# Last group of a two-layer kernel: block 0 from halves, blocks 1 and 2 through partial rows in DRAM, eight first products copied into the other bank

## The chip, the cores and the metric

The kernel runs on one core of a Trainium2 chip. Its engines run side by side, each with its own queue of instructions taken in order: TensorE (PE in the rows, its weight loads PEld), VectorE (DVE), ScalarE (ACT), GpSimd (POOL) and SyncE (SP). SP and POOL issue DMAs; the 16 DMA engines of the core carry them out. The metric is the device time of one execution in microseconds, the median of several runs.

## The reference

```
state = gamma * state + outer(k_t, v_t);  y_t = scale * q_t @ state      # 2 batches, 8 heads, 768 steps, 64 wide
x = y as 1536 tokens x 512                                               # float32 throughout
h = x @ w_in (512 x 2048);   g = h * clip(h + 3, 0, 6) / 6;  x = g @ w_out (2048 x 512)
h = x @ w_in2;               g = h * tanh(softplus(h));      out = g @ w_out2
```

The two matrix layers make up nearly all of the arithmetic. Their first products are x @ w_in, their second products g @ w_out.

## The kernel before

Everything is held transposed: features on the 128 partitions, tokens along the row. The 1536 tokens are three blocks (0, 1, 2) of 512. The 2048 inner features are 16 tiles of 128, two tiles to a pair, two pairs to a group: four groups, 0 to 3, in each layer. A float32 factor is split into a high and a low part (`gh` and `gl`, or `wbh1` and `wbl1` for every third one, on the operand side; `wdh`, `wdl` or the sums in `sb` on the weight side), and a product is three passes on TensorE: high by high, low by high, high by low.

Blocks 1 and 2 together, and the two halves of block 0 by themselves, are multiplied by a scheme of seven products in place of eight; the names end in 1 to 7. `up_pair` makes the first products. For blocks 1 and 2 (`who` is "w") product 1 goes into a PSUM bank `wx`, ScalarE copies it to SBUF (`snap`), product 2 goes into a bank `wy`, and VectorE adds that bank to the copy (`plus`, line 933, the task `c11`), ahead of the activation function.

The second products of a group come in one of three forms. `pair_down` handles blocks 1 and 2 by seven products for each of two pairs and two output tiles: 84 matmuls of 512 columns. `block_down` handles block 0 plainly: 48 matmuls of 512 columns (the last three of them cut in two). `half_down` handles block 0 by its two halves, with the seven products: 84 matmuls of 256 columns. The tuple `HD` names the groups of layer 1 whose block 0 is taken from halves: groups 1 and 2. Group 3, the last one, takes `pair_down` first and then `block_down`.

The groups of layer 1 add up. In groups 0 to 2 ScalarE copies a finished bank to a row tile in SBUF (`copied`, line 1057), and a DMA brings that tile into `part`, a tensor in DRAM of 3 blocks by 4 output tiles of 128 x 512: the first time with a plain write by SP, afterwards with an accumulating DMA issued by POOL (`into_part`, line 1071). There are eight row tiles, taken in turn. In group 3 `read_back` loads all twelve tiles of `part` into SBUF (`xah` and `xal` for blocks 1 and 2, `xch` for block 0), VectorE adds each bank to its tile (`into_back`, line 1063), and SP stores the sums to the output (line 1098). A row of blocks 1 and 2 is stored when its last product is in.

What stands where in each engine's queue is set by a planner (`Plan.order`): for the first part of the program by a written list of names (`SEQ`), after that greedily, by costs and ranks that are constants of the file. So an edit in one place changes the order of neighbouring work elsewhere. Each tile of SBUF or PSUM is handed out in the planned order, and a wait stands where one engine needs what another made.

Of the kernel before, what the change touches and what calls it, by code (L numbers as in the profile page):

```python
# [23 lines left out]
P = 128  # L24
# [8 lines left out]
TB = UPB * P  # L33

NG = 4
# [32 lines left out]
ORDER = (1, 5, 6, 3, 7, 2, 4)  # L68
WP = (1,)
PG = (1, 2)  # L70
HD = (1, 2)
MORE = True
APART = 2
DEFER = {11: 5}
# [177 lines left out]
def body(ctx: ExitStack, tc: tile.TileContext, aps: dict, out: bass.AP):  # L252
    nc = tc.nc
# [639 lines left out]
    def up_pair(who, layer, p):  # L893
        X, Z, Y = wk("x"), wk("y"), wk("y")
        nm = f"{who}{layer}_{p}"
        forms = tform[layer, who]
        if who == "w":
            pass_us, first, last = MMR, slice(0, TB), slice(0, TB)
            g11, g12, g21, g22 = [gbuf(layer, 2 * p + k, b) for k in range(2) for b in (1, 2)]
        else:  # L900
            pass_us, first, last = MMH, slice(0, TB // 2), slice(TB // 2, TB)
            g11, g21 = [gbuf(layer, 2 * p + k, 0) for k in range(2)]
            g12, g22 = g11, g21
        n = first.stop

        def product(k, ps, start, cols, extra):
            l, r = PROD[k]
            which, q = LHS[l]
            if which == 0:
                lh, ll, _ = wbase[layer, 2 * p]  # L910
                ldeps = wbase[layer, 2 * p][2] + wbase[layer, 2 * p + 1][2]
            else:
                lh, ll, lt = wsum[layer, p]
                ldeps = [lt]
            (rh, rhk, rht), (rl, rlk, rlt), rdeps = forms[r]

            def run():
                m = 0
                for kc in range(2):
                    ws = slice(256 * q + kc * P, 256 * q + (kc + 1) * P)  # L920
                    xh, xl = rh.tile[:, rhk.start + kc, rht], rl.tile[:, rlk.start + kc, rlt]
                    for a, c in ((lh, xh), (ll, xh), (lh, xl)):
                        mm(ps.tile[:, cols], a.tile[:, ws], c, start and m == 0, m == 5)
                        m += 1
            return add(f"P{k}_{nm}", "PE", 6 * pass_us, ldeps + rdeps + extra,
                       list(dict.fromkeys([lh, ll, rh, rl, ps])), run, pe_rank[who, layer, p, k])

        def snap(k, ps, pc, gb, gc, dep):
            return add(f"s{k}_{nm}", "ACT", act(n), [dep] + (att_tasks if gb.tag[:2] == "gs" else []), [ps, gb],
                       lambda: A.copy(gb.tile[:, gc], ps.tile[:, pc]))  # L930

        def plus(k, ps, pc, gb, gc, deps):
            return add(f"c{k}_{nm}", "DVE", dve(n), deps, [ps, gb], lambda: V.tensor_tensor(
                out=gb.tile[:, gc], in0=ps.tile[:, pc], in1=gb.tile[:, gc], op=ALU.add),
                pe_rank[who, layer, p, {11: 2, 12: 3, 22: 7}[k]] + 6 * pass_us + (FREE0 if p < NP and who == "w" and k == 11 else FREE) if layer == 1 else None)
        ahead = []
        if layer == 0 and who == "v" and p // NP in PG and p // NP % 2 and p % NP == 0:
            ahead = [up_t["w", 0, p + NP - 1, k] for k in (2, 3, 4)]
        p1 = product(1, X, True, first, ahead)
        s1 = snap(1, X, first, g11, first, p1)  # L940
        if seq_of(who, layer, p) == EARLY_Y:
            p2 = product(2, Y, True, first, [p1])
            p5 = product(5, Z, True, last, [p2])
        else:
            p5 = product(5, Z, True, last, [p1])
            p2 = product(2, Y, True, first, [p5])
        s5 = snap(5, Z, last, g22, last, p5)
        c11 = plus(11, Y, first, g11, first, [p2, s1])
        p6 = product(6, X, False, first, [s1, p1])
        s2 = snap(2, X, first, g12, last, p6)  # L950
        p3 = product(3, Z, False, last, [s5, p5])
        c12 = plus(12, Z, last, g12, last, [p3, s2])
        p7 = product(7, X, False, first, [s2])
        c22 = plus(22, X, first, g22, last, [p7, s5])
        p4 = product(4, X, False, first, [c22])
        f = 2 * p
        if who == "w":
            gval[layer, f, 1] = (g11, [mish_or_swish(f"{layer}_{f}_1", layer, g11, [c11])])
            gval[layer, f, 2] = (g12, [mish_or_swish(f"{layer}_{f}_2", layer, g12, [c12])])
            gval[layer, f + 1, 2] = (g22, [mish_or_swish(f"{layer}_{f + 1}_2", layer, g22, [c22])])  # L960
            gval[layer, f + 1, 1] = (g21, [mish_or_swish(f"{layer}_{f + 1}_1", layer, g21, [p4], src=X)])
        else:
            gval[layer, f, 0] = (g11, [mish_or_swish(f"{layer}_{f}_0", layer, g11, [c11, c12])])
            gval[layer, f + 1, 0] = (g22, [mish_or_swish(f"{layer}_{f + 1}_0d", layer, g22, [c22], last),
                                           mish_or_swish(f"{layer}_{f + 1}_0c", layer, g22, [p4], first, X)])
        for k, t in ((1, p1), (2, p2), (3, p3), (4, p4), (5, p5), (6, p6), (7, p7)):
            up_t[who, layer, p, k] = t
# [67 lines left out]
    back = {}  # L1035
    spares, landed = {}, {}

    def copied(layer, nm, ac, dep, rk):
        if layer not in spares:
            own = [buf("fix", [P, 512], f"sb0{d}") for d in range(4)]  # L1040
            if layer == 0:
                pass
            else:
                wide = buf("fix", [P, 1024], "q")
                own += [buf("fix", [P, 512], "t"), buf("fix", [P, 512], "qc"), View(wide, 0, 512), View(wide, 512, 512)]
            spares[layer] = own
        tp = spares[layer][taken[0] % len(spares[layer])]
        taken[0] += 1
        if layer:
            before = sum([tform[1, w][n][2] for w in "wv" for n in ("T1", "T2", "T3", "T4")], [])  # L1050
        else:
            before = []
            if tp not in spares[layer][:4]:
                before = sum([tform[0, w][n][2] for w in "wv" for n in ("T1", "T2", "T3", "T4")], [])
        sc = 1.0 if layer else 1.0 / 6.0
        return tp, add(f"ev{layer}{nm}", "ACT", act(512), [dep, landed.get(tp)] + before, [ac, tp],
                       lambda: A.activation(tp.tile, ac.tile, AF.Copy, scale=sc), rk)  # L1057
# [14 lines left out]
                out=pt.tile, in_=tp.tile, accum_op=ALU.add))  # L1072

    def read_back(b):
        whole = buf("fix", [P, 2048], ("xch", "xah", "xal")[b])
        for d in range(4):
            v = View(whole, 512 * d, 512)
            pt = part[1, b, d]
            back[b, d] = (v, [add(f"pr{b}_{d}", "SP", 0.8, [added[1, b, d]], [v, pt], lambda v=v, pt=pt:
                                  nc.sync.dma_start(out=v.tile, in_=pt.tile))])  # L1080
# [21 lines left out]

    def pair_down(g, layer=1):
        ps = range(g * NP, (g + 1) * NP)
        final = layer == 1 and g == NG - 1
        pd, z = ("pd", "") if layer else ("pd0", "0")
        gt, gd, sd = {}, {}, {}
        if layer == 0 and g == 2 and MORE:
# [42 lines left out]
        for k in ORDER:  # L1151
# [21 lines left out]
            for d in range(2):  # L1173
                ac, rk, nm = accs[banks[k][d]], rank_after(k, d), f"{z}{g}_{k}_{d}"
                dd = 2 * half + d
                if final:
                    into_back(nm, ac, b, dd, [last[d]], rk, k in (3, 7, 2, 4))
                    ev[banks[k][d]] = back[b, dd][1] if k not in (3, 7, 2, 4) else []
                elif k == 3:
                    tp, t = kept[d]  # L1180
                    t = joined(nm, ac, tp, slice(0, 512), [last[d], t], rk, None if layer else 1.0 / 6.0)
                    into_part(layer, nm, tp, b, dd, t)
                else:
                    tp, t = copied(layer, nm, ac, last[d], rk)
                    ev[banks[k][d]] = [t]
                    if k == 6:
                        kept[d] = (tp, t)
                    else:
                        into_part(layer, nm, tp, b, dd, t)

    def half_down(g):
        ps = range(g * NP, (g + 1) * NP)
# [13 lines left out]
        def form(k):  # L1206
# [6 lines left out]
            for p, c in zip(ps, hs):  # L1213
# [14 lines left out]
                prev_split[0] = a  # L1228
                seen[p, n] = [low[-1]]
            return gh, gl, low  # L1230
        free = sum([tform[1, w][n][2] for w in "wv" for n in ("T1", "T2", "T3", "T4")], [])
        accs, last, ev = {}, {}, {}
        banks = {k: (0, 1) if k in (1, 6, 7, 4) else (2, 3) for k in ORDER}
# [128 lines left out]
    for g in range(NG):  # L1362
        for key in flow1[g]:
            need(key)
        if g == NG - 1:
            for b in (1, 2, 0):
                read_back(b)
        for what in AFTER[g]:
            (pair_down if what == "p" else half_down if g in HD else block_down)(g)

# [71 lines left out]
```

## Time and profile before

| | |
|---|---|
| median of 3 runs | 530.24 us (529.26 to 533.11) |
| profiled execution, its own time | 528.86 us |
| its span, first to last instruction | 527.1 us |
| TensorE busy | 521.0 us, 99% of the span |
| VectorE busy | 447.2 us, 85% |
| ScalarE busy | 356.0 us, 68% |
| GpSimd busy | 58.0 us, 11% |
| granted TensorE clock | 0.998 of full speed |
| DMA, mean | 150 GB/s |

A busy share says how long an engine had an instruction in hand. Matmuls overlap, so their distance from start to start is the price of one, not their duration. VectorE and ScalarE instructions overlap a little with their neighbours too. The share of the DMA engines is the time that their packets took, over 16 engines; it can pass 1 when packets overlap.

### The profile page before, as it was taken

The numbers are of one execution on the slowest core, as the hardware profiler recorded it, in microseconds if no ns is written. First come the engines' busy times: TensorE is split into PE (matmuls) and PEld (weight loads), VectorE is DVE, ScalarE is ACT, GpSimd is POOL, SyncE is SP. The second block draws the span as 40 slices with busy tenths as digits, with TensorE's granted clock in tenths as the row PEclk, the third lists the DMA queues.
The fourth block names the chain that finished last, engine by engine and source line by source line (L and its number), as shares of the span: only waits on it lengthen the run. The fifth ranks groups of instructions, "written<-read, shape, count | busy, mean of one in ns | idle before, by whom it ended". The sixth has DMA issues, their size and how long they took to land.

```text
span 527.1 us, 8602 instructions
## 1 busy us (share of the span) xinstructions
PE 521.0 (99%) x3186; PEld 444.7 (84%) x3186; DVE 447.2 (85%) x745; ACT 356.0 (68%) x646; POOL 58.0 (11%) x70
## 2 busy tenths in 40 slices
PE   8999999999999999999999999999999999999996
PEld 5888888888889888888888898888998899888885
DVE  4999998799998969778889999977899879987892
ACT  3488496757786666686655777776768778786540
POOL 1000000001330020340000000020024300540000
PEclk9999999999999999999999999999999999999999
DMA  8995115443994362798530024682149941995532
GB/s 329 406 410 196 29 52 168 159 156 92 175 193 124 134 139 35 147 127 267 195 130 2 0 81 140 220 199 100 63 116 150 241 133 32 183 123 116 188 137 105
DMA packets 27179, 78.92 MB, mean 150 GB/s; under 512 B 3024, under 2 KB 4432, under 8 KB 27136
## 3 DMA queue, kind: packets, MB, share of 16 engines
q1 hardware_dynamic: 17920, 61.58, 32.3%
q0 software_dynamic: 9216, 16.78, 22.1%
q8 instruction: 25, 0.41, 0.3%
q14 instruction: 18, 0.15, 0.1%
HBM read 52.13 MB, written 26.21 MB: 149 GB/s over the span
## 4 chain that ended last, share of the span: by engine, by line
PE 97%; DMA 1%; DVE 1%; issue 0%; DVEq 0%
PE acc L285 50%; PE wx L285 26%; PE wy L285 21%; DMA kv<-in_kv_dram 1%; DVE A L687 0%; DVE vp L680 0%; DVE xch L1063 0%; DVEq L1437 0%; DVE t L494 0%; DVE bias L266 0%; DVEq L680 0%
## 5 line engine op out<-in xcount | busy, mean ns | idle before, releaser
L285 PE MATMUL acc<-gh,wdl 128*128 128x512 f32 (+1 forms) x216 | 82.6, 382 | 0.0
L285 PE MATMUL acc<-gh,wdh 128*128 128x512 f32 (+1 forms) x216 | 82.5, 382 | 0.0
L285 PE MATMUL acc<-gl,wdh 128*128 128x512 f32 (+1 forms) x216 | 82.3, 381 | 0.0
L1071 POOL DMA_DIRECT2D part<-sb x42 | 37.6, 937 | 387.9 <-ACT sb L1057 294.5
L285 PE MATMUL acc<-gh,sb 128*128 128x512 f32 (+1 forms) x204 | 57.1, 365 | 0.0
L285 PEld LDWEIGHTS acc<-gl,wdh 128*128 128x128 f32 x216 | 40.6, 188 | 7.9
L612 DVE TENSOR_TENSOR cv<-cv 128x256 f32<-128x256 f32 x108 | 45.5, 422 | 1.6
L285 PEld LDWEIGHTS acc<-gh,wdh 128*128 128x128 f32 x216 | 40.7, 188 | 7.2
L285 PEld LDWEIGHTS acc<-gh,wdl 128*128 128x128 f32 x216 | 40.7, 188 | 7.1
L979 ACT CAST gh<-g 128x512 fp32r<-128x512 f32 x54 | 33.5, 621 | 18.0 <-PE acc L285 13.7
L981 DVE TENSOR_TENSOR gl<-g,gh 128x512 fp32r<-128x512 f32 x54 | 37.2, 688 | 9.8 <-PE acc L285 4.8
L285 PEld LDWEIGHTS acc<-gh,sb 128*128 128x128 f32 x204 | 36.5, 189 | 5.9
L554 DVE SCALAR_TENSOR_TENSOR cv<-raw,top 128x1024 int32<-128x1024 int32 (+1 forms) x34 | 39.3, 1157 | 0.4 <-ACT top L549 0.2
L285 PE MATMUL acc<-gl,sb 128*128 128x512 f32 (+1 forms) x102 | 37.1, 364 | 0.0
L979 ACT CAST gh<-gs 128x512 fp32r<-128x512 f32 x43 | 26.7, 620 | 14.9 <-PE acc L285 14.1
L1057 ACT ACTIVATE sb<-acc 128x512 f32<-128x512 f32 x52 | 30.9, 600 | 6.5 <-PE acc L285 5.7
L549 ACT ACTIVATE top<-raw 128x1024 f16<-128x1024 bf16 (+1 forms) x25 | 32.1, 1283 | 1.1 <-DMA raw<-in_w_dram 1.1
L981 DVE TENSOR_TENSOR gl<-gs,gh 128x512 fp32r<-128x512 f32 x43 | 29.6, 688 | 3.4 <-ACT gh L979 2.8
L565 DVE SCALAR_TENSOR_TENSOR wdl<-cv,wdh 128x512 fp32r<-128x512 f32 x32 | 21.6, 686 | 7.6 <-ACT wdh L563 7.3
L285 PE MATMUL wy<-xbh,wsh 128*128 128x512 f32 x60 | 23.5, 392 | 0.0
L285 PE MATMUL wy<-xbh,wsl 128*128 128x512 f32 x60 | 23.4, 390 | 0.0
L285 PE MATMUL wx<-q,wsh 128*128 128x512 f32 x60 | 23.3, 389 | 0.0
(252 smaller groups left out, 1459.0 us busy)
## 6 DMA issues: line engine op xcount, KB each, us to landing
raw<-in_w_dram SPq DMA_DIRECT2D x30, 1023.8 KB, 4.8
part<-sb POOLq DMA_DIRECT2D x42, 256.0 KB, 5.0
qk<-in_qk_dram SPq DMA_DIRECT2D x12, 512.0 KB, 7.3
kv<-in_kv_dram SPq DMA_DIRECT2D x10, 516.0 KB, 6.4
part<-sb SPq DMA_DIRECT2D x18, 256.0 KB, 2.1
part<-q POOLq DMA_DIRECT2D x10, 256.0 KB, 4.9
q<-part SPq DMA_DIRECT2D x8, 256.0 KB, 6.1
raw<-in_w_dram SPq DMA_DIRECT2D x4, 511.8 KB, 7.9
```

The lines of the kernel that those rows point to most:

```text
L285: nc.tensor.matmul(o, l, r, start=start, stop=stop, skip_group_check=True)
L549: a1 = add(nm + "t", "ACT", act(n) * 1.33, [ld, top_free[0]], [rb, t_b], lambda: A.activation(top(), high(), AF.Copy, scale=0.5))
L554: top_free[0] = add(nm + "o", "DVE", dve(n), [a1], [rb, t_b, cb], lambda: V.scalar_tensor_tensor(out=cb.tile.bitcast(I32)[:, cs], in0=low( ...
L565: return add(nm + "lo", "DVE", dve(n), [a], list(dict.fromkeys([cb, hb, lb])), lambda: V.scalar_tensor_tensor(out=lb.tile[:, l0:l0 + n], i ...
L612: prev = [add(nm + f"s{o}", "DVE", dve(256), prev, [cb], lambda o=o, x=x, y=y, op=op: V.tensor_tensor(out=q(o), in0=q(x), in1=q(y), op=op))]
L979: a = add(f"hi{nm}", "ACT", act(512), deps + [prev_split[0]], [gb, gh], lambda: A.copy(gh.tile, gb.tile))
L981: lambda: V.tensor_tensor(out=gl.tile, in0=gb.tile, in1=f32(gh.tile), op=ALU.subtract))
L1057: lambda: A.activation(tp.tile, ac.tile, AF.Copy, scale=sc), rk)
L1071: landed[tp] = added[layer, b, d] = add(f"pa{nm}", "POOL", ADDED, [dep, added[layer, b, d], *more], [tp, pt], lambda: nc.gpsimd.dma_start( ...
```

## The change

Three edits. First, `HD` gains group 3: the second products of block 0 in the last group are made by `half_down`, whose branch for the last group adds each 128 x 256 bank to the tile that was read back into `xch` and stores half rows. Second, `pair_down` loses its branch for the last group: blocks 1 and 2 of group 3 go the way of the other groups, by ScalarE copies and accumulating DMAs into `part`, and SP then copies each finished tile of `part` from DRAM to the output in DRAM; only block 0 is read back. Third, for the eight pairs of layer 0 and layer 1 in `ONTO`, product 1 is copied by ScalarE into the `wy` bank instead of SBUF, product 2 is accumulated onto it by TensorE, and the VectorE addition is gone; the activation function reads the bank.

```diff
+ONTO = ((0, 2), (0, 3), (0, 5), (0, 6), (0, 7), (1, 3), (1, 5), (1, 7))
-HD = (1, 2)
+HD = (1, 2, 3)
...
+        onto = who == "w" and not early and ((layer, p) in ONTO)
...
-        s1 = snap(1, X, first, g11, first, p1)
+        s1 = snap(1, X, first, Y if onto else g11, first, p1)
...
-            p2 = product(2, Y, True, first, [p5])
+            p2 = product(2, Y, not onto, first, [p5] + ([s1] if onto else []))
...
-        c11 = plus(11, Y, first, g11, first, [p2, s1])
+        c11 = p2 if onto else plus(11, Y, first, g11, first, [p2, s1])
...
-            gval[layer, f, 1] = (g11, [mish_or_swish(f"{layer}_{f}_1", layer, g11, [c11])])
+            gval[layer, f, 1] = (g11, [mish_or_swish(f"{layer}_{f}_1", layer, g11, [c11], src=Y if onto else None)])
...
-        whole = buf("fix", [P, 2048], ("xch", "xah", "xal")[b])
+        whole = buf("fix", [P, 2048], "xch")
...
-        final = layer == 1 and g == NG - 1
...
-                if final:
-                    into_back(nm, ac, b, dd, [last[d]], rk, k in (3, 7, 2, 4))
-                    ev[banks[k][d]] = back[b, dd][1] if k not in (3, 7, 2, 4) else []
-                elif k == 3:
+                if k == 3:
...
+                if layer and g == NG - 1 and k in (3, 7, 2, 4):
+                    pt = part[1, b, dd]
+                    add(f"y{nm}", "SP", 0.8, [added[1, b, dd]], [pt], lambda b=b, dd=dd, pt=pt: nc.sync.dma_start(
+                        out=out[dd * P:(dd + 1) * P, b * TB:(b + 1) * TB], in_=pt.tile))
...
-            for b in (1, 2, 0):
-                read_back(b)
+            read_back(0)
```

On SP, at the end of the program, before (the reads of `part` in its last four rows, then the stores of sums):

```order
L1080 DMA xah_5149<-part_340_3696 128x512
L1080 DMA xch_5243<-part_335_3474 128x512
L1080 DMA xch_5243<-part_336_3493 128x512
L1080 DMA xch_5243<-part_334_3464 128x512
L1098 DMA out_dram<-xal_5152 128x512 x4
L1098 DMA out_dram<-xah_5149 128x512 x4
L1098 DMA out_dram<-xch_5243 128x512 x3
L1098 DMA out_dram<-xch_5243 128x256 x2
```

The same place now; a `part` row is a tile of blocks 1 or 2 that goes from DRAM to DRAM, an `xch` row a half row of block 0:

```order
L1086 DMA xch_5225<-part_336_3488 128x512
L1194 DMA out_dram<-part_341_3607 128x512
L1194 DMA out_dram<-part_342_3614 128x512
L1194 DMA out_dram<-part_343_3539 128x512
L1277 DMA out_dram<-xch_5225 128x256 x2
L1194 DMA out_dram<-part_337_3507 128x512
L1277 DMA out_dram<-xch_5225 128x256 x4
L1194 DMA out_dram<-part_344_3547 128x512
L1277 DMA out_dram<-xch_5225 128x256 x2
L1194 DMA out_dram<-part_338_3517 128x512
L1194 DMA out_dram<-part_339_3687 128x512
L1194 DMA out_dram<-part_340_3691 128x512
```

Eight reads of `part` into SBUF are gone, the eight stores of blocks 1 and 2 have become eight copies between DRAM tensors, and three of these stand behind the last half rows.

On POOL the queue ended with group 2's accumulations; now twelve more follow, the last eight of them these (`t`, `qc`, `q` and `sb` are the row tiles):

```order
L1077 DMA part_341_3607<-t_3497 128x512
L1077 DMA part_342_3614<-qc_3503 128x512
L1077 DMA part_343_3539<-q_3526 128x512
L1077 DMA part_337_3507<-sb_732_3443 128x512
L1077 DMA part_344_3547<-q_3526 128x512
L1077 DMA part_338_3517<-sb_733_3453 128x512
L1077 DMA part_339_3687<-sb_734_3461 128x512
L1077 DMA part_340_3691<-sb_735_3473 128x512
```

Each of these eight is followed by one copy on SP that waits for it to land.

On VectorE, the last work of the program before (L1063 adds a bank, L981 makes a low part):

```order
L981 TENSOR_TENSOR wbl_989_5396<-wsh_942_4737,wbh_988_5389 128x512
L981 TENSOR_TENSOR gl_5407<-wsh_942_4737,gh_5402 128x512
L1063 TENSOR_TENSOR xah_5149<-acc_950_5106,xah_5149 128x512
L1063 TENSOR_TENSOR xah_5149<-acc_951_5178,xah_5149 128x512
L981 TENSOR_TENSOR gl_5422<-wsl_946_5183,gh_5414 128x512
L981 TENSOR_TENSOR wbl_995_5441<-wsl_946_5183,wbh_994_5436 128x512
L1063 TENSOR_TENSOR xch_5243<-acc_986_5410,xch_5243 128x512
L1063 TENSOR_TENSOR xch_5243<-acc_987_5417,xch_5243 128x512
```

A stretch of the same work now (L1272 adds a bank, L1232 makes a low part, L1210 a difference of the operands):

```order
L1272 TENSOR_TENSOR xch_5225<-acc_986_5422,xch_5225 128x256
L1232 TENSOR_TENSOR gl_5495<-wsh_942_5105,gh_5479 128x256
L1272 TENSOR_TENSOR xch_5225<-acc_987_5438,xch_5225 128x256
L1210 TENSOR_TENSOR wsh_942_5105<-wsh_942_5105 128x256
L1232 TENSOR_TENSOR gl_5495<-wsl_946_5174,gh_5479 128x256
L1210 TENSOR_TENSOR wsl_946_5174<-wsl_946_5174 128x256
L1272 TENSOR_TENSOR xch_5225<-acc_982_5402,xch_5225 128x256
L1232 TENSOR_TENSOR wbl_1001_5528<-wsh_942_5105,wbh_1000_5512 128x256
```

Block 0 takes 36 operations of 256 columns (8 differences, 14 low parts, 14 additions) in place of nine (four low parts and five additions, two of these of 256 columns); the additions for blocks 1 and 2 in group 3 have left VectorE but for two.

## Rows read from the trace of the kernel before

**Rows 1.** The page: busy time by engine, and the chain's shares by engine.
```profile
PE 521.0 (99%) x3186; PEld 444.7 (84%) x3186; DVE 447.2 (85%) x745; ACT 356.0 (68%) x646; POOL 58.0 (11%) x70
PE 97%; DMA 1%; DVE 1%; issue 0%; DVEq 0%
```

**Rows 2.** Waits of TensorE, whole span: total us, times, longest us.
```profile
PE acc L285 <- DVE t L494: 1.2, 1, 1.2
PE acc L285 <- DVE vp L680: 0.3, 1, 0.3
PE wy L285 <- DVE A L687: 0.2, 1, 0.2
```

**Rows 3.** Chain that ended last, in order of time, its last long piece: start, us.
```profile
495.05 27.95 PE acc L285 x126
```

**Rows 4.** Timeline of TensorE: last product of blocks 1, 2; block 0's first and last.
```profile
511.69 0.39 PE L285 MATMUL acc<-gl,wdh 128*128 128x512 f32 x1
511.92 0.39 PE L285 MATMUL acc<-wbh,wdh 128*128 128x512 f32 x1
...
522.59 0.28 PE L285 MATMUL acc<-wbh,wdl 128*128 128x256 f32 x1
522.71 0.28 PE L285 MATMUL acc<-wbl,wdh 128*128 128x256 f32 x1
```

**Rows 5.** Page, costliest groups: ScalarE copies of a finished bank.
```profile
L1057 ACT ACTIVATE sb<-acc 128x512 f32<-128x512 f32 x52 | 30.9, 600 | 6.5 <-PE acc L285 5.7
```

**Rows 6.** Groups of VectorE by shape: additions of a `wy` bank.
```profile
L933 DVE TENSOR_TENSOR gs<-wy,gs 128x512 f32<-128x512 f32 x15 | 10.3, 689 | 4.5 <-PE wy L285 3.1 <-ACT gs L850 0.7 <-PE acc L285 0.7
L933 DVE TENSOR_TENSOR g<-wy,g 128x512 f32<-128x512 f32 x15 | 10.3, 688 | 5.7 <-PE wy L285 5.7
```

**Rows 7.** Timeline of VectorE: two neighbours of 256 columns, in group 2's halves.
```profile
437.33 0.42 DVE L1204 TENSOR_TENSOR wsl<-wsl 128x256 f32<-128x256 f32 x1
437.66 0.42 DVE L1204 TENSOR_TENSOR wsh<-wsh 128x256 f32<-128x256 f32 x1
```

**Rows 8.** Timeline of VectorE and SP at the end, then the window behind the last transfer.
```profile
523.02 0.76 DVE L1063 TENSOR_TENSOR xch<-acc,xch 128x256 f32<-128x256 f32 x2
523.03 1.33 SPq L1098 DMA_DIRECT2D out_dram<-xch  x3
526.00:527.10 1.10, 0.00 (x0) 0.00 (x0) 0.00 (x0) 0.00 (x0) 0.00 (x0) 0.50 0.00 0
```

**Rows 9.** Page, DMA queues (packets, MB, share) and issues (count, KB, us to landing).
```profile
q0 software_dynamic: 9216, 16.78, 22.1%
part<-sb POOLq DMA_DIRECT2D x42, 256.0 KB, 5.0
```

**Rows 10.** DMA queue of POOL in 470 to 476 us, then 422.5 to 424.5 us.
```profile
q0 software_dynamic: 474, 0.86, 103.1%
...
q0 software_dynamic: 205, 0.39, 106.7%
```

**Rows 11.** One accumulating DMA with nothing ahead of it, issued at 466.98 us.
```profile
part<-t POOLq DMA_DIRECT2D x1, 256.0 KB, 4.0
```

**Rows 12.** DMA queue of SP: 484 to 492 (loads), 504 to 516 (stores), 521 to 527.1.
```profile
q1 hardware_dynamic: 1008, 1.84, 70.6%
...
q1 hardware_dynamic: 1146, 2.09, 47.0%
out_dram<-xal SPq DMA_DIRECT2D x4, 256.0 KB, 2.0
...
q1 hardware_dynamic: 720, 1.05, 47.8%
```

**Rows 13.** Both DMA queues busy at once: 410 to 412 us, then 418 to 422 us.
```profile
q1 hardware_dynamic: 85, 0.70, 100.1%
q0 software_dynamic: 3, 0.00, 0.7%
...
q1 hardware_dynamic: 115, 0.94, 72.6%
q0 software_dynamic: 112, 0.20, 28.2%
```

More of the change, by code (lines that the diff above doesn't have):

```diff
@@ L904, in up_pair @@
         n = first.stop
+        early = seq_of(who, layer, p) == EARLY_Y
+        onto = who == "w" and not early and ((layer, p) in ONTO)
         def product(k, ps, start, cols, extra):
@@ L939, in up_pair @@
         p1 = product(1, X, True, first, ahead)
-        s1 = snap(1, X, first, g11, first, p1)
-        if seq_of(who, layer, p) == EARLY_Y:
+        s1 = snap(1, X, first, Y if onto else g11, first, p1)
+        if early:
             p2 = product(2, Y, True, first, [p1])
@@ L1036, in body, with spare @@
     spares, landed = {}, {}
-    def copied(layer, nm, ac, dep, rk):
+    def spare(layer):
         if layer not in spares:
@@ L1046, in copied @@
             spares[layer] = own
+    def copied(layer, nm, ac, dep, rk):
+        spare(layer)
         tp = spares[layer][taken[0] % len(spares[layer])]
@@ L1230, in form @@
             return gh, gl, low
+        spare(1)
         free = sum([tform[1, w][n][2] for w in "wv" for n in ("T1", "T2", "T3", "T4")], [])
```

## The prediction

> **What bounds the kernel now.** I read the busy shares and the chain first: TensorE is busy 99% of the span, and the chain that ended last is TensorE for 97% [rows 1]. A busy share could hide small stalls, so the waits come next: TensorE waited 1.7 us in all, three times, all of it at the start of the program [rows 2]. From start to start the matmuls stand 0.227 us apart at 512 columns and 0.12 us at 256, to the end [rows 4]. So until its last matmul this kernel is TensorE's instruction count; an edit gains there only if it takes matmuls away. Behind it lies a tail: the last matmul starts at 522.71 [rows 4], VectorE's last additions run to 523.78, SP's last store issues at about 523.9 (three issues in 1.33 us, 0.44 us each) and the last transfer has ended by 526.0; 1.1 us without any work closes the span [rows 8]. The chain's last piece covers blocks 1 and 2 and then block 0 of the last group without a gap [rows 3]. I set t = 0 at 511.92, where block 0 begins [rows 4]; the products before it keep their number, so I leave this point where it is. In t, TensorE ends at 10.9, the transfers at 14.1, the span at 15.2.
>
> **The first products onto copied banks.** Eight VectorE additions of 0.69 us go [rows 6], 5.5 us; no matmul comes or goes. VectorE was not what TensorE waited for, so this is worth 0 at the end; what hides it is TensorE's own unbroken work. The new wait: product 2 now needs ScalarE's copy. In the new order of TensorE 18 to 120 matmuls of 512 columns' worth stand between the two in each of the eight places, at least 4.08 us of work by 0.227 us each, and a copy of a bank takes 0.6 us [rows 5]. A copy from bank to bank shows in no row; below zero it cannot gain, and were it three times as slow it would still fit. Behind product 2 all of TensorE would wait, so ScalarE more than 3 us late would cost its lateness. I take 0, with 0 to 2 us for all eight. The `wy` banks are held longer, and the planner has moved neighbouring products for that; I keep the same 0 to 2 us for that.
>
> **Block 0 from halves.** Before: 45 matmuls of 0.227 us and 6 of 0.12 us, 10.9 us. After: 84 of 0.12 us, 10.1 us. TensorE ends at t = 10.1: 0.8 us gained, if it is fed. Feeding: VectorE has 36 operations of 256 columns, 0.335 us from start to start [rows 7], 12.1 us, against 10.1 us on TensorE. It must start early: the operand buffers are three deep, so the first half's low part can start when the third product from the end has been read, 2.7 us before t = 0, and ScalarE's cast (about 0.4 us) is done: t = -2.2. Then VectorE ends at 9.9 at the soonest, and its last addition, which waits for the last matmul, at 10.6. Each half product finds its operands by a margin of tenths. Without the head start TensorE would wait some 2 us. I take 0.1 us; bounds 0 and 2 us.
>
> **Blocks 1 and 2 through `part`.** Eight reads into SBUF go (they ran from 484 us, under TensorE: worth 0), twelve additions of 0.69 us become ScalarE copies of 0.6 us [rows 5]: two to a product of 2.7 us, next to two casts of 0.62 us, so ScalarE keeps up. New are twelve accumulating DMAs and, behind each of the last eight, a copy from DRAM to DRAM.
>
> *When they are issued.* Six products after the first one take 16.3 us up to t = 0, so the banks are copied at about t = -16.3, -15.1 and -13.6, -12.4 (products 1, 5), then at -7.5, -6.9 (3), -5.5, -4.3 (7), -2.7, -1.8 (2) and 0.0, 0.8 (4).
>
> *What one costs.* 9216 packets are 64 accumulating DMAs, 144 each [rows 9]. With only these in hand the DMA engines carried 474 packets in 6 us, 1.82 us for 144, and with a deeper backlog 205 in 2 us, 1.4 us [rows 10]. With its issue, an undisturbed one lands after 4.0 us [rows 11], so its packets start some 1.75 us behind the issue. Here a backlog builds; I take 1.6 us between these two. A load from `part` cost 70.6% of 8 us for 7, 0.81 us; a store of the same size 47.0% of 12 us for 8, 0.71 us; by the last window a half row costs 0.4 us [rows 12]. DRAM to DRAM is in no row. From below it is bounded by the store, 0.71 us (a gain is excluded: it moves the same bytes); from above by the accumulation, 1.82 us, which also reads and writes DRAM. I take the load's 0.81 us, since it is plain and reads DRAM.
>
> *The sum.* The first four accumulations are over by t = -7. From -5.7 on the DMA engines have 8 x 1.6 + 8 x 0.81 + 8 x 0.4 = 22.5 us of work: end at t = 16.8, 17.2 with the last receipt. TensorE and the half rows are done by then: the last half row can be issued at 11.1, three copies behind it at 11.6, 12.0 and 12.5 if their accumulations have landed. So the DMA engines become the bound of the tail.
>
> *How two queues share.* Where both had work, SP's queue carried 85 packets and POOL's 3 in 2 us, but 115 and 112 in another 4 us [rows 13]: once SP's first, once in turns. In turns, the copies thread between the accumulations and the sum above holds: 17.2. If SP's transfers go first, the last accumulation lands last, and its copy follows alone (issue, 0.81 us, receipt): about 18.8. I take 17.5, nearer the first, for the packets here are of one size as in no window of rows 13. The Trainium skill says, in DMA: Bandwidth & Descriptors (Queues, rings and completion order), that each DMA engine goes round its queues packet by packet; by this rule alone the end is 17.2, and the first window of rows 13 does not agree with it.
>
> Result: the span ends at 511.9 + 17.5 + 1.1 = 530.5, 3.4 us later than 527.1. The profiled execution took 528.86 us by its own time, 1.4 us under the median of 530.24; I add the 3.4 us to both: 532.3 for such an execution, **533.6 us** for the median.
>
> **The rivals.** *DMA keeps up* (0.21). Accumulations at 1.4 us and copies at 0.71 us leave 8 x 1.4 + 8 x 0.71 + 3.2 = 20.1 us of work, over at t = 14.4; then the half rows and the three copies behind them set the end: eight transfers of 4.3 us in all, issued from 9.3 on, end at 15.1 to 15.5. Span 528.5, median 531.6; 530.2 if the copies land like stores. For it: a backlog raises the rate. Against it: 1.82 us was the rate in the group just before. The Trainium skill's formula for POOL's DMAs (the same page, Anatomy of one DMA: about 2.0 us plus the bytes over 436 GB/s) gives 2.6 us for a tile, and by it nothing would pile up. An undisturbed landing of 4.0 us [rows 11] is over that.
>
> *Slower: copies or accumulations are dear* (0.26). At 1.82 us for an accumulation with SP's transfers first the end is t = 20.5; with copies at the accumulation's price too, 8 x 1.82 x 2 + 3.2 = 32.3 us from -5.7 give 27. Span 533.5 to 540, median 536.6 to 543. It decides from about 1.1 us a copy at 1.6 us an accumulation. For it: DRAM is read and written at once, and SP's first window. Against it: loads and stores side by side reach 0.7 to 0.8 us.
>
> *TensorE is starved in the halves or at a copied bank* (0.06): 1 to 4 us there. The DMA engines get that time for their backlog, so the end moves less than 2 us: 534 to 536.
>
> *Faster* (0.02): the eight additions were holding something up; 5.5 us and 0.8 us go, 524. No wait in rows 2 speaks for it.
>
> **How the numbers follow.** One per cent, 5.3 us, is about what a measurement of this kernel tells from no change: 524.9 and 535.5 are the bounds. The forecast's own case has 0.45, with 531.6 to 535.5 around 533.6. Slower by over 1%: the dear transfers, 0.26, a third of the starved case, 0.02, and 0.03 from the forecast's upper edge: 0.31. Faster 0.02, within 0.67. The range holds the forecast, most of the first rival, and the second up to copies of 1.3 us: 530.2 to 539.
>
> **What would show it.** Right: in the profile after, TensorE ends near 522 without gaps behind 495, the DMA share stays near 1 from 506 to 529, POOL's last accumulation lands some 12 us after its issue, and the chain ends with a `part` to `out_dram` copy on SP. Wrong: the DMA share falls before 524 and SP's last issue is at 524 (first rival); copies that land 4 us and more after their issue with nothing else in flight (second); gaps on TensorE behind 512 that wait for a low part (third).

## The result and the profile after

The changed kernel took 533.26 us (median of 14 runs, 532.81 to 534.68), the kernel before 529.23 us beside it (14 runs); the ratio is 1.0074, 95% interval 1.0061 to 1.0088. Forecast were 533.6 us, and 3.4 us more than before; it became 3.9 us more by the ratio. The profiled execution took 532.84 us with a span of 531.0 us, against 528.86 and 527.1. So the time was inside the range and near the forecast, in part by luck: the kernel before came out 1.0 us under the 530.24 us that the forecast stood on, and the increase 0.5 us over the forecast one, so the two misses partly cancel. Whether the reason was right is another question, and the experiments answer it differently.

The page of the changed kernel: busy time by engine, and the chain's shares. Then TensorE's waits over the whole span.

```profile
PE 520.6 (98%) x3219; PEld 445.6 (84%) x3219; DVE 443.3 (83%) x752; ACT 364.2 (69%) x668; POOL 68.7 (13%) x82
PE 96%; DMA 1%; DVE 1%; issue 0%; DVEq 0%
```

```profile
PE acc L286 <- DVE t L495: 1.2, 1, 1.2
PE acc L286 <- DVE vp L681: 0.3, 1, 0.3
PE wy L286 <- DVE A L688: 0.2, 1, 0.2
```

Against [rows 1] VectorE has 3.9 us less, ScalarE 8.2 us more, TensorE almost the same. The waits are those of [rows 2] to the tenth: nothing new in 500 us (gaps shorter than these are not in that view). TensorE's timeline around block 0, to set against [rows 4]:

```profile
511.75 0.39 PE L286 MATMUL acc<-gl,wdh 128*128 128x512 f32 x1
512.15 0.38 PE L286 MATMUL acc<-wbh,wdh 128*128 128x256 f32 x1
512.37 0.28 PE L286 MATMUL acc<-wbh,wdl 128*128 128x256 f32 x1
...
522.16 0.28 PE L286 MATMUL acc<-wbh,wdl 128*128 128x256 f32 x1
522.28 0.28 PE L286 MATMUL acc<-wbl,wdh 128*128 128x256 f32 x1
```

Block 0 starts at 512.15, 0.23 us later than before; 0.17 us of it is a gap ahead of the first half matmul (0.40 us behind the one before it in place of 0.227). From the first to the last start pass 10.13 us, and TensorE is through 0.43 us sooner than before. The loss lies behind it. SP's queue from there on (start, time of the group, count):

```profile
518.32 1.12 SPq L1277 DMA_DIRECT2D out_dram<-xch  x2
519.49 0.50 SPq L1194 DMA_DIRECT2D out_dram<-part  x1
520.43 2.37 SPq L1277 DMA_DIRECT2D out_dram<-xch  x4
522.89 0.50 SPq L1194 DMA_DIRECT2D out_dram<-part  x1
523.48 1.02 SPq L1277 DMA_DIRECT2D out_dram<-xch  x2
524.75 2.06 SPq L1194 DMA_DIRECT2D out_dram<-part  x3
```

Before, the last issue was over at 524.36 [rows 8] and the last packet by 525.7, 1.3 us behind it (the first window below). Now the last issue is over at 526.81 (+2.45) and the last packet ends 3.0 us behind it (+1.7): 529.8. Windows behind TensorE, first before, then now, with the DMA share in the column before the last; then SP's wait at the very end:

```profile
525.70:526.00 0.30, 0.00 (x0) 0.00 (x0) 0.00 (x0) 0.00 (x0) 0.00 (x0) 0.50 0.00 0
...
526.80:529.80 3.00, 0.00 (x0) 0.00 (x0) 0.00 (x0) 0.00 (x0) 0.00 (x0) 0.50 0.81 256
529.80:531.00 1.20, 0.00 (x0) 0.00 (x0) 0.00 (x0) 0.00 (x0) 0.00 (x0) 0.50 0.00 0
```

```profile
SPq L1443 <- DMA out_dram<-part: 2.4, 3, 1.2
```

The end is the landing of the three copies that SP issued last. The page's own chain stops at VectorE's last addition and does not show this; SP's waits do.

The DMA queues from 506 to 530 us hold just the eight accumulations, the eight copies and the eight half rows (packets, MB, share):

```profile
q0 software_dynamic: 1152, 2.10, 61.1%
q1 hardware_dynamic: 2304, 3.15, 39.6%
```

POOL's queue carried 14.7 us of packets, 1.83 us an accumulation; SP's 9.5 us, against the 9.7 us of the forecast's prices. In the sum 24.2 us, and the share stays near 1 up to 529. Read by itself, this is the forecast's picture.

### The profile page after: what moved, and what is told of

Same layout as the page of the kernel before. It is cut to its first block, busy times and chain, and to the rows that moved or that the text cites. A ratio compares the mean times of both kernels' runs of the same rounds, so it can differ in the third digit from the quotient of the medians.

```text
span 531.0 us, 8725 instructions
## 1 busy us (share of the span) xinstructions
PE 520.6 (98%) x3219; PEld 445.6 (84%) x3219; DVE 443.3 (83%) x752; ACT 364.2 (69%) x668; POOL 68.7 (13%) x82
## 4 chain that ended last, share of the span: by engine, by line
PE 96%; DMA 1%; DVE 1%; issue 0%; DVEq 0%
PE acc L286 50%; PE wx L286 26%; PE wy L286 21%; DMA kv<-in_kv_dram 1%; DVE A L688 0%; DVE xch L1272 0%; DVE vp L681 0%; DVE t L495 0%; DVE bias L267 0%; DVEq L681 0%
## 5 line engine op out<-in xcount | busy, mean ns | idle before, releaser
L1077 POOL DMA_DIRECT2D part<-sb x50 | 44.4, 955 | 419.6 <-ACT sb L1063 315.1
L286 PE MATMUL acc<-gh,wdl 128*128 128x512 f32 (+1 forms) x212 | 80.6, 380 | 0.0
L286 PE MATMUL acc<-gh,wdh 128*128 128x512 f32 (+1 forms) x212 | 80.6, 380 | 0.0
L286 PE MATMUL acc<-gl,wdh 128*128 128x512 f32 (+1 forms) x212 | 80.4, 379 | 0.0
L286 PE MATMUL acc<-gh,sb 128*128 128x512 f32 (+1 forms) x228 | 61.6, 356 | 0.0
L286 PEld LDWEIGHTS acc<-gh,sb 128*128 128x128 f32 x228 | 40.3, 189 | 5.9
L286 PE MATMUL acc<-gl,sb 128*128 128x512 f32 (+1 forms) x114 | 40.5, 356 | 0.0
L1063 ACT ACTIVATE sb<-acc 128x512 f32<-128x512 f32 x60 | 35.7, 599 | 6.6 <-PE acc L286 5.3
L982 ACT CAST gh<-gs 128x512 fp32r<-128x512 f32 x43 | 26.6, 619 | 13.0 <-PE acc L286 12.5
L286 PEld LDWEIGHTS acc<-gl,sb 128*128 128x128 f32 x114 | 21.5, 189 | 3.1
```

What stands on the lines that cost most here:

```text
L286: nc.tensor.matmul(o, l, r, start=start, stop=stop, skip_group_check=True)
L982: a = add(f"hi{nm}", "ACT", act(512), deps + [prev_split[0]], [gb, gh], lambda: A.copy(gh.tile, gb.tile))
L1077: landed[tp] = added[layer, b, d] = add(f"pa{nm}", "POOL", ADDED, [dep, added[layer, b, d], *more], [tp, pt], lambda: nc.gpsimd.dma_start( ...
```

## The experiments

For a common measure I count from block 0's first matmul on TensorE to the end of the span. The start of the program varies by some us between executions (TensorE's first waits), and this takes it out. Before: 511.92 to 527.1, 15.2 us; changed: 512.15 to 531.0, 18.85 us. These are single profiled executions; the ratios of the experiments to the kernel before come from five rounds each.

| kernel | ratio to before (95%) | block 0's start, span | start to end |
|---|---|---|---|
| changed | 1.0074 (1.0061 to 1.0088) | 512.15, 531.0 | 18.85 |
| banks alone | 0.9991 (0.9982 to 1.0001) | 512.65, 527.7 | 15.05 |
| halves alone | 0.9994 (0.9984 to 1.0003) | 513.09, 527.7 | 14.6 |
| rows alone | 1.0086 (1.0072 to 1.0100) | 512.93, 532.4 | 19.5 |
| onto the output | 0.9969 (0.9958 to 0.9980) | 512.19, 525.9 | 13.7 |
| onto the output, no banks | 0.9969 (0.9952 to 0.9987) | 512.73, 526.4 | 13.7 |
| onto the output, plain block 0 | 0.9990 (0.9971 to 1.0010) | 512.81, 527.8 | 15.0 |
| half copies | 1.0059 (1.0038 to 1.0080) | 513.27, 530.4 | 17.1 |
| last copies on ScalarE | 1.0067 (1.0051 to 1.0083) | 513.55, 531.4 | 17.85 |
| plain writes | 1.0075 (1.0057 to 1.0093) | 513.86, 532.6 | 18.7 |
| plain writes, last copies on ScalarE | 1.0035 (1.0018 to 1.0051) | 512.33, 529.5 | 17.2 |
| plain writes, copies first | 0.9989 (0.9977 to 1.0001) | 514.97, 529.0 | 14.0 |
| copies of block 1 only | 1.0059 (1.0040 to 1.0078) | 512.61, 530.4 | 17.8 |

### Which of the three edits

**Banks alone.** The old last group, with `ONTO` kept:

```diff
-HD = (1, 2, 3)
+HD = (1, 2)
...
+                if final:
+                    into_back(nm, ac, b, dd, [last[d]], rk, k in (3, 7, 2, 4))
...
+            for b in (1, 2, 0):
+                read_back(b)
```

> Only the eight first products go onto copied banks; the last group is as before. My theory (the time went to the DMA engines in the tail): no change, ratio to before 0.998 to 1.002, span 527.1 within 0.5 us, TensorE without waits after the start. Rival (the copied banks or the new order of products cost TensorE time): a ratio over 1.003, with gaps on TensorE ahead of a second product.

Measured: 0.9991, no change. Its span is 0.6 us longer than that of before, 0.1 us more than I had allowed, with a wait of TensorE of 0.8 us for an input at the start that the execution of before did not have. The eight copied banks and the moved products are worth nothing that shows.

**Halves alone.**

```diff
-ONTO = ((0, 2), (0, 3), (0, 5), (0, 6), (0, 7), (1, 3), (1, 5), (1, 7))
+ONTO = ()
...
+                if final:
+                    into_back(nm, ac, b, dd, [last[d]], rk, k in (3, 7, 2, 4))
...
+            for b in (1, 2, 0):
+                read_back(b)
```

> Only block 0 of the last group is made from halves; blocks 1 and 2 are read back and joined as before. My theory: TensorE ends 0.4 us sooner, as it does in the changed kernel (522.56 in place of 522.99), the last half row is issued by about 523.6 and lands 2.0 us later, then 1.1 us: span 526.7, ratio 0.998 to 1.000. Rival (VectorE starves TensorE in the halves, and this is a part of the loss): TensorE ends after 523.5 and the ratio is over 1.002.

Measured: 0.9994, and 14.6 us from the start of block 0 in place of 15.2. From 513.09 to 524.07, where its last matmul starts, TensorE took 11.0 us, not 10.1, and no less than the 10.8 us of plain block 0 [rows 4]: eleven matmuls started about 0.1 us late, against two in the changed kernel.

```profile
524.07 0.28 PE L286 MATMUL acc<-wbl,wdh 128*128 128x256 f32 x1
```

So the rival's sign came true on TensorE (it ends after 523.5), the rival's ratio did not, and what is gained lies behind TensorE. Here VectorE still adds the banks of blocks 1 and 2; that this starves the halves is likely but not shown. The ratio is in the expected range, its interval holds 1: no loss is here, and a gain of half a us can't be told from none.

**Rows alone.**

```diff
-ONTO = ((0, 2), (0, 3), (0, 5), (0, 6), (0, 7), (1, 3), (1, 5), (1, 7))
-HD = (1, 2, 3)
+ONTO = ()
+HD = (1, 2)
```

> Only blocks 1 and 2 of the last group go through the partial rows and are copied to the output; block 0 stays plain, nothing goes onto copied banks. My theory (the tail is the DMA engines' work): the whole loss is here, span 530.4 to 531.2, ratio 1.006 to 1.009. Rival (the loss needs the eight half rows that stand between the copies on SP's queue): five stores in place of eight take two thirds of it away, ratio under 1.004.

Measured: 1.0086, span 532.4: the whole loss, and no less than with the half rows. SP's last groups:

```profile
524.39 1.55 SPq L1104 DMA_DIRECT2D out_dram<-xch  x3
526.04 1.78 SPq L1194 DMA_DIRECT2D out_dram<-part  x3
```

Five stores of block 0 or eight, three copies stand behind them.

### The copies taken away

**Onto the output.** The rows of blocks 1 and 2 of layer 1 are the output's own rows, from the first write of group 0 on:

```diff
+    for b in (1, 2):
+        for d in range(4):
+            part[1, b, d] = Buf(f"out{b}{d}", lambda b=b, d=d: out[d * P:(d + 1) * P, b * TB:(b + 1) * TB])
...
-                if layer and g == NG - 1 and k in (3, 7, 2, 4):
-                    pt = part[1, b, dd]
-                    add(f"y{nm}", "SP", 0.8, [added[1, b, dd]], [pt], lambda b=b, dd=dd, pt=pt: nc.sync.dma_start(
-                        out=out[dd * P:(dd + 1) * P, b * TB:(b + 1) * TB], in_=pt.tile))
```

> The changed kernel with the rows of blocks 1 and 2 of layer 1 held in the output tensor itself: the same accumulating DMAs, but onto the output, and the eight copies from DRAM to DRAM are gone. My theory: the DMA engines have the accumulations (14.7 us of packets from 506.5 on) and the half rows (3.2 us), over at about 523.5 to 524; the last half row sets the end as in the kernel without the rows: span 526.5 to 527.3, ratio 0.998 to 1.001, over 3.5 us faster than the changed kernel. Rival (the accumulations alone bound the tail): the last one lands after 525.5 and the span is 528 or more, ratio over 1.002.

Measured: 0.9969, faster than both kernels, 1.6 us under the kernel before; 13.7 us from block 0's start. POOL's queue from 506 to 524, and SP's last group:

```profile
q0 software_dynamic: 1152, 2.10, 83.3%
```

```profile
518.35 5.24 SPq L1276 DMA_DIRECT2D out_dram<-xch  x8
```

The accumulations cost the same (15.0 us of packets for eight), and yet the tail is shorter than before: the half rows set the end, as expected. It was 0.6 us better than the lower end of my span, and the ratio lies under the range that I gave. This tells that the copies make the loss, not how: by their work or by their place.

**Onto the output, with plain block 0, and without the banks.** The same edit with

```diff
-HD = (1, 2, 3)
+HD = (1, 2)
```

> As the kernel that accumulates onto the output itself, but with block 0 of the last group plain, as before the change. What the half products are worth when the copies are gone: my theory says 0.4 us at TensorE's end and nothing in the tail, so a span of 526.3 to 527.0 against 525.9, ratio to before 0.997 to 0.9995. Rival (the gain of that kernel comes from the half rows being smaller at the very end): span 527.0 or more, ratio 0.9995 or over.

and with

```diff
-ONTO = ((0, 2), (0, 3), (0, 5), (0, 6), (0, 7), (1, 3), (1, 5), (1, 7))
+ONTO = ()
```

> The kernel that accumulates onto the output itself, with the eight first products copied to SBUF and added by VectorE again, as before the change. My theory (the eight additions are off the path): ratio to before 0.996 to 0.999, from block 0's first matmul to the end 13.7 us within 0.4, as with the copied banks. Rival (VectorE needs the 5.5 us to feed the halves): TensorE waits in block 0, ratio 0.9995 or over.

Measured: 0.9990 (0.9971 to 1.0010) with plain block 0, at 15.0 us from its start, and 0.9969 without the banks, at 13.7 us. So the halves are worth about 1.3 us once the copies are gone: 0.7 us on TensorE, the rest behind it. My 0.4 us was too small: the span of 527.8 us is where the rival had it, the ratio where I had it, and the interval touches that of the kernel with the halves. The banks are worth nothing here either.

### By their work or by their place

**Half copies.**

```diff
-                        out=out[dd * P:(dd + 1) * P, b * TB:(b + 1) * TB], in_=pt.tile))
+                        out=out[dd * P:(dd + 1) * P, b * TB:b * TB + 256], in_=pt.tile[:, 0:256]))
```

> The changed kernel with every copy from DRAM to DRAM cut to 256 of its 512 columns: the other half of the rows of blocks 1 and 2 is never written to the output. My theory (work of the DMA engines, in proportion): the eight copies fall from 6.4 us of packets to about 3.2, the span from 531.0 to 528.0 (527.4 to 528.8), ratio to before 1.001 to 1.004. Rival (a chain of latencies: each copy takes its 3.5 to 4 us behind an accumulation's receipt, whatever its size): span 530.4 to 531.2, ratio over 1.006.

Measured: 1.0059, 17.1 us. Neither theory: SP's packets fell from 9.5 to 6.7 us, 2.8 us of work, the time by 1.7 us. SP's queue in 506 to 530 us, then in 526 to 528 us, while the last copies ran:

```profile
q1 hardware_dynamic: 2304, 2.10, 27.8%
...
q1 hardware_dynamic: 358, 0.33, 50.2%
```

With the DMA engines half idle, work no longer bounds that end. What was saved is mostly the landing of a last copy, 2.5 us from its issue in place of 3.9 us.

**Last copies on ScalarE.**

```diff
-                    add(f"y{nm}", "SP", 0.8, [added[1, b, dd]], [pt], lambda b=b, dd=dd, pt=pt: nc.sync.dma_start(
+                    late = k == 4 or k == 2 and d == 1
+                    add(f"y{nm}", "ACT" if late else "SP", 0.1 if late else 0.8, [added[1, b, dd]], [pt], lambda b=b, dd=dd, pt=pt, late=late: (nc.scalar if late else nc.sync).dma_start(
```

> The changed kernel with its last three copies, those that stood behind the last half rows on SP's queue, issued from ScalarE's queue behind its last cast; nothing else is moved. My theory (the DMA engines have no free time between 506 and 529): no gain, span 530.5 to 531.5, ratio to before 1.006 to 1.009. Rival (SP's order holds them back: they were issued at 524.75 to 526.3, up to 2.5 us after their rows had landed): issued by 524, landed by 528, span 528.5 to 529.5, ratio under 1.005.

Measured: 1.0067, as my theory said, but 1.0 us shorter from block 0's start. The copies, then the last half rows, and what SP waited for there:

```profile
521.55 3.38 ACTq L1195 DMA_DIRECT2D out_dram<-part  x3
...
526.87 0.81 SPq L1278 DMA_DIRECT2D out_dram<-xch  x2
```

```profile
SPq L1278 <- DMA out_dram<-xch: 1.1, 1, 1.1
SPq L1278 <- DMA out_dram<-part: 1.0, 1, 1.0
```

Counted from block 0's start, the three copies were all issued by 11.4 us in place of 14.7; now the half rows were last, held by transfers that had not landed. The Trainium skill says, in DMA: Bandwidth & Descriptors (Issuing engines are not separate DMA queues), that issuing on several engines saves only the sequencer's time; this run's ratio agrees, 1.0067 against 1.0074. The same move with plain writes, below, saves more (1.0035 against 1.0075), since it takes the copies from behind half rows that wait for the end; so the sequencer's time is not all that it can save.

**Plain writes.** What became of the main term of my sum, if the accumulations are made cheap:

```diff
-                out=pt.tile, in_=tp.tile, accum_op=ALU.add))
+                out=pt.tile, in_=tp.tile, **({} if nm.startswith("3_") else {"accum_op": ALU.add})))
```

> The changed kernel with the twelve transfers of the last group's rows into the partial rows as plain writes in place of accumulating ones, on the same queue of POOL: the sums of the first three groups are lost for blocks 1 and 2. If the price of an accumulation, 1.83 us of packets, is that DRAM is read and written, a plain write costs 0.7 to 0.8 us like a store, the eight fall by 8 us and the tail is bound by issue and receipt: span 527 to 528.5, ratio to before 0.999 to 1.003. If it is POOL's queue or its 144 packets that cost, nothing changes: 531.0, ratio 1.006 to 1.009.

Measured: 1.0075, 18.7 us. That looks like the second answer, but the trace says otherwise. POOL's queue from 505 to 533, its last issue, and SP's last group:

```profile
q0 software_dynamic: 640, 2.10, 20.6%
```

```profile
515.00 0.54 POOL L1077 DMA_DIRECT2D part<-sb  x1 [0.25 <-ACT gh L1231]
...
526.06 2.08 SPq L1194 DMA_DIRECT2D out_dram<-part  x3
```

Eight transfers took 5.8 us of packets in place of 14.7 (80 packets each, not 144), the last was issued at 515.00, and still the end did not move: 8.9 us of the work that my sum of 22.5 us was made of are gone, for 0.1 us. So that sum alone does not hold the end of the changed kernel. SP's order is enough to hold it: the last three copies were issued behind the last half rows, their rows landed by 519.6. Nor do the accumulations make these copies land later. Their times from issue to landing, in the changed kernel and here:

```profile
DMA to landing us min/median/max: 3.8/3.9/4.1
DMA to landing us min/median/max: 3.5/3.7/4.1
```

**Plain writes, last copies on ScalarE.** Both edits above together; the diff is theirs.

> Both earlier edits at once: the last group's rows go into the partial rows by plain writes (the sums of the first three groups are lost for blocks 1 and 2), and the last three copies are issued from ScalarE's queue. Counted from block 0's first matmul on TensorE the span ended after 18.85 us in the changed kernel, 18.7 with plain writes alone, 17.85 with the three copies moved alone. My theory now (two bounds that lie close together, either of which holds the end: SP's order, with three copies behind the last half rows, and the work of the DMA engines, which the accumulations make up in the main): only with both lifted does the time come back, to 15.0 to 16.0 us, ratio to before 0.999 to 1.003. Rival (a copy between DRAM tensors is late by its own latency wherever it is issued): 17.5 or more, ratio over 1.004.

Measured: 1.0035, 17.2 us, between the two answers. The copies on ScalarE's queue, and the DMA engines in 518 to 520 us:

```profile
520.34 1.95 ACTq L1195 DMA_DIRECT2D out_dram<-part  x3
```

```profile
q1 hardware_dynamic: 143, 0.13, 19.7%
```

The rows lay ready by 518.5, the DMA engines were nearly idle, and the copies stood behind ScalarE's last cast: held by place once more, then bunched with the half rows. The edit had not lifted the bound it was to lift.

**Plain writes, copies first.** The edit of the plain writes, and all eight copies ahead of the half rows on SP:

```diff
-                    add(f"y{nm}", "SP", 0.8, [added[1, b, dd]], [pt], lambda b=b, dd=dd, pt=pt: nc.sync.dma_start(
+                    t = add(f"y{nm}", "SP", 0.8, [added[1, b, dd]], [pt], lambda b=b, dd=dd, pt=pt: nc.sync.dma_start(
...
+                    t.after = ld_last[0]
+                    ld_last[0] = t
...
-                        add("y" + nm, "SP", 0.5, [t], [v], lambda v=v, dd=dd, c=c: nc.sync.dma_start(
+                        y = add("y" + nm, "SP", 0.5, [t], [v], lambda v=v, dd=dd, c=c: nc.sync.dma_start(
...
+                        y.after = ld_last[0]
```

> Plain writes of the last group's rows (the sums of the first three groups are lost for blocks 1 and 2) and all eight copies put ahead of the half rows on SP's queue, so that no copy waits for block 0. The copies then run as soon as their rows have landed, by about 8 us after block 0's first matmul. If place and time of issue set the end and not the copies as such, the end is that of the kernel without copies, 13.7 to 15.2 us after block 0's first matmul, ratio to before 0.997 to 1.001. If copies are dear wherever they stand: 17 us or more, ratio over 1.003.

Measured: 0.9989, 14.0 us. SP's queue:

```profile
509.88 11.67 SPq L1195 DMA_DIRECT2D out_dram<-part  x8
521.65 4.99 SPq L1280 DMA_DIRECT2D out_dram<-xch  x8
```

The same eight copies, all of them done before the first half row has landed, cost next to nothing: 14.0 us against 13.7 without any. This is shown with plain writes only.

**Copies of block 1 only.** Block 2's rows accumulate onto the output; block 1's keep their copies:

```diff
+    for b in (2,):
+        for d in range(4):
+            part[1, b, d] = Buf(f"out{b}{d}", lambda b=b, d=d: out[d * P:(d + 1) * P, b * TB:(b + 1) * TB])
...
-                if layer and g == NG - 1 and k in (3, 7, 2, 4):
+                if layer and g == NG - 1 and k in (2, 4):
```

> The changed kernel with block 2's rows accumulated onto the output itself, so that its four copies are gone; block 1's four rows keep the partial rows and their copies, the ones that stand last on SP. Counted from block 0's first matmul to the end of the span the changed kernel took 18.85 us, and 13.7 us without any copy. If a copy costs by its work, half the copies are half the loss: 16.3 us, ratio to before 1.001 to 1.003. If the last copies set the end by their place (behind the last accumulation and the last half rows on SP, three issues and the landing of the last), nearly all of it stays: 17.5 to 18.5 us, ratio 1.004 to 1.008.

Measured: 1.0059, 17.8 us: half the copies gone, 80% of the loss still there (17.8 less 13.7 of 18.85 less 13.7). SP's last two groups:

```profile
523.68 1.00 SPq L1280 DMA_DIRECT2D out_dram<-xch  x2
524.78 1.14 SPq L1197 DMA_DIRECT2D out_dram<-part  x2
```

Two copies behind the last half rows are enough to hold the end.

## Why the prediction was right, and where its reason was not

**Banks: right.** Worth 0, in two settings (0.9991 alone; 0.9969 with and without them in the kernel without copies).

**Halves: right in the sum, small in the end.** TensorE takes 10.13 us from first to last start, about 10.25 with the last matmul's own 0.12 (10.1 and 0.1 for waits forecast), and ends 0.43 us sooner, 0.17 us being lost in a gap ahead of the first half matmul. The gain is hidden behind the copies.

**Prices: copy and half row right, accumulation short.** Eight copies and eight half rows took 9.5 us of packets (9.7 forecast). An accumulation took 1.83 us, the upper bound, not 1.6: the backlog did not raise the rate.

**Two queues: in turns, as taken.** While both had transfers on their way they carried about as many packets each. In 512 to 514 us:

```profile
q0 software_dynamic: 96, 0.18, 69.3%
q1 hardware_dynamic: 91, 0.17, 26.0%
```

**Issue of the accumulations: wrong.** I had the last banks copied at t = 0 and 0.8 and the accumulations issued at once, so that the last would land some 12 us after its issue. The copies ended at 512.10 and 512.88, as forecast, but POOL issued at 516.51 and 518.49 (ScalarE's last copies, then POOL's last issues, then the last landing in us from its issue):

```profile
511.50 0.60 ACT L1063 ACTIVATE sb<-acc 128x512 f32<-128x512 f32 x1 [0.40 <-PE acc L286]
512.28 0.60 ACT L1063 ACTIVATE sb<-acc 128x512 f32<-128x512 f32 x1
```

```profile
512.12 0.86 POOL L1077 DMA_DIRECT2D part<-sb  x1 [0.41 <-ACT sb L1063]
516.51 0.86 POOL L1077 DMA_DIRECT2D part<-sb  x1 [3.53 <-ACT gh L1231]
518.49 0.88 POOL L1077 DMA_DIRECT2D part<-sb  x1 [1.11 <-ACT gh L1231]
```

```profile
part<-sb POOLq DMA_DIRECT2D x1, 256.0 KB, 5.4
```

From the end of its copy to its landing, at 523.9, the last accumulation took 11.0 us, about what was forecast; but half of this it stood on POOL, and it landed 5.4 us after its issue, not 12. With plain writes POOL issued these two 0.4 us after their copies, at 514.21 and 515.00.

**The sum: the number was right, the bound was not the one that came last.** The step that failed is "From -5.7 on the DMA engines have 22.5 us of work", and with it "So the DMA engines become the bound of the tail". With 8.9 us of that work taken out the end stayed (18.7 against 18.85 us); with the copies put ahead of the half rows as well it came back to 14.0. What comes last is the order on SP: the last addition ends at 523.02, two half rows are issued by 524.50, then three copies, 2.06 us, the last at about 526.3, 2.4 us after its row had landed; it lands 3.9 us after its issue (the row below, its last value), and 0.8 us close the span. These steps lead to 531.0 without any sum of work. The prediction had this chain too, with the last copy issued at t = 12.5, and set it aside as done by then. It came at t = 14.1 (counted from block 0's start at 512.15) and landed 3.9 us later, where a store takes 2.0 [rows 12].

```profile
out_dram<-part SPq DMA_DIRECT2D x1, 256.0 KB, 3.9
```

The two bounds lie close together, which is why the sum gave nearly the right time: with the three copies taken off SP the end came only 1.0 us sooner, now with the last half rows waiting for transfers that landed late. The gap between plain writes and accumulations in that setting, 17.2 against 17.85 us in the profiled executions and 1.0035 against 1.0067, is what the accumulations then cost. Luck has a part too: at the measured prices the sum is 24.2 us and its work ends at t = 18.5, 0.9 us after the last packet did (529.8), so the price that was too low brought the forecast nearer. With accumulations, copies ahead of all the half rows were not tried: the last row lands at 523.9, and eight half rows would stand behind it. By an estimate from these rows (t = 11.7 for that landing, 3.0 to 3.9 us for a copy to land, 0.8 us to close) no order of SP brings this kernel under 15.5 to 16.4 us; how much of the loss the accumulations hold by themselves stays open.

**Rivals.** DMA keeps up (531.6) had the mechanism that came last, the half rows and the three copies behind them, but too low: it had these transfers end at t = 15.1 to 15.5, and the last packet came at 17.65. With plain writes, where the DMA engines do keep up (a share of 0.80 to 0.82 from 526 to 530), the end is the same. Dear transfers: not the copies, 0.8 us each; the accumulations did cost what that rival took, 1.83 us. Starved TensorE: 0.17 us. Of the signs named, the share near 1, TensorE's end and the copy on SP at the end (in SP's waits, not in the page's chain) came true, the 12 us did not; agreement of the share with the forecast was no proof, since it is also what a full queue looks like while something else sets the end.

## What to carry to other kernels

In a tail, write down for each queue what stands behind what, and add issue and landing times along it, before summing work: a transfer that was ready long ago can still be the last if it stands behind one that waits for the end. When a forecast's number comes out right, take away its largest term and see whether the time moves. A sum that was to end in an output tensor can be accumulated there from the start: this kernel then needs no copies, and with the halves it is the fastest here, 527.94 us against 529.61 us, ratio 0.9969.

## What the runs showed of the hardware

- **POOL held its accumulations back with three on their way.** In the changed kernel the fifth, sixth, seventh and eighth of the last eight were issued at 510.83, 512.12, 516.51 and 518.49, each 0.3 to 0.4 us after the one three places ahead had landed (505.38 + 5.1, 507.06 + 4.8, 509.78 + 6.4, 510.83 + 7.3). For the last two, the program's only wait is for ScalarE's copy, done over 4 us before. The kernel that accumulates onto the output shows the same (514.34 after 509.82 + 4.2). With plain writes it was not so: the last of eight was issued at 515.00 with four on their way (the first of these, 511.49 + 3.7, landed behind it). What holds the accumulations is not shown.
- **A plain write from POOL took 80 packets and 0.72 us, the accumulation 144 packets and 1.83 us**, its issue 0.54 us against 0.87. The price is the accumulation's, not that of POOL's queue; how much of it is reading, and how much the packets, is open.
- **A copy between DRAM tensors costs 0.80 us of packets, like a load, but lands late:** 3.0 us from its issue with little else in flight (in the kernel with plain writes, issued at 521.18), against 2.0 us for a store of the same size [rows 12].
